# Holding back the last free buffer only when a transpose will soon need it

## The chip, the cores and the metric

The kernel runs on one core of a Trainium2 chip. The metric is the device time of one execution in microseconds; lower is better.

## What is computed

Four blocks follow one another on eight batch rows of one token each (448 features): attention A, mixer B, attention A, mixer B, with the same weights both times. Cut to what matters:

```python
q = (layernorm(x) @ wq)                       # 16 query heads of 256
scores = einsum("bhqd,bhkd->bhqk", q, k) * 256 ** -0.5   # 8 cached heads, 4096 keys, each for 2 query heads
o = einsum("bhqk,bhkd->bhqd", softmax(scores), v)
x = x + o @ wo                                # A
y = layernorm(x); x1 = y + mixed(gelu(layernorm(y) @ w1)) @ w2   # B; one token: the mixed part is zero
x = x + x1 + gelu(layernorm(x1) @ w3) @ w4
```

With one token a row, every shift in the mixing part shifts in zeros, so that term vanishes and `w1` and `w2` are not read. What is large is the cache: keys and values, 8 batch rows x 8 heads x 4096 x 256 in bf16 each.

## The kernel before

**Units, steps, parts.** A unit `t` is (pass, batch row, head): pass 1 is the first attention, pass 2 the second. `units` lists 144 of them in a hand-made order, gaps included: for each batch row the pass 1 heads, then a stretch with two gaps in which the dense layers between the attentions run (`mid_steps`, one piece a step), then at a unit called the fence the pass 2 heads. Each unit has four steps, `q` = 0 to 3, and the step number is `i = 4 * t + q`. A head's keys and values are cut in four parts of 512 KB each.

**Slots.** SBUF holds 31 slots of 512 KB (`slots`, parts of the tile `slab`). A part of K is loaded into a slot, transposed on VectorE from that slot into another one (`transposes`, two instructions at L562), and scored from there on TensorE (`k_part`, L653). A part of V is loaded and multiplied by the softmax weights (`v_part`, L630). The transposed keys of six heads a batch row stay in their slots from pass 1 to pass 2, except for two parts that are parked in PSUM (L567) and copied back by ScalarE (L520). So a K part takes one slot more for the time of its transpose, and gives back the slot it was loaded to.

**The list of loads.** `loads` is worked out beforehand: parts of K at the pace of `by`, parts of V at the step of their use in `plan` (some six steps after the unit's scores). `pump` takes loads from it while more than `RESERVE` = 1 slots are free, and issues them on SyncE's queue (L536). Two parts that follow each other go as one transfer of 1 MB, where the list and `take_two` allow it; where the pair can't be had and enough is under way, `pump` returns and waits for a pair of free slots. `pump` runs whenever a slot comes free: after a transpose, after the scores of a part that isn't kept, after a part of V. All of this happens while the program is built: on the chip, only the engines' orders and their waits are left, and a load waits for the last reader of its slot.

**Transposes.** At step `i`, `transposes` works off `todo` up to the number `by[i]`. A part that is not scored yet at this step can be put off: where it isn't loaded or no slot is free, the function returns and tries again at the next step.

**The softmax of a unit.** VectorE's reduce at L668 after the last scores, a broadcast on TensorE (L676), VectorE's reduce of the maximum at L686, exponentials on ScalarE (L689), sums and a reordering on TensorE (L702, L712), ScalarE's copies to `pt` (L720), VectorE's sum at L727 and a power on GpSimd (L731). These stand in the engines' orders among transposes, scores and values, at fixed steps.

Of the kernel before, what the change touches and what calls it, by code (L numbers as in the profile page):

```python
# [15 lines left out]
UNIT = 2048  # L16
N_SLOTS = 31
RESERVE = 1
KEEP = 6
PARKED = 2  # L20
RUN = 2
# [10 lines left out]
def kernel(  # L32
# [164 lines left out]
    def flush():  # L197
        while between:
            between.pop(0)()
# [162 lines left out]

    heads = list(range(G))
    loose = heads[: G - KEEP]

# [30 lines left out]
    def fresh(u, s):  # L398

        return u is not GAP and (u[0] == 1 or u[2] in loose)  # L400
# [4 lines left out]
    t = 0  # L405
# [21 lines left out]
    parts = [(t, s) for t in range(n_units) for s in range(4) if fresh(units[t], s)]  # L427
# [16 lines left out]
    for t in order:  # L444
        for s in range(4):
            i = late_v.get((t, s), 4 * t + s + LAG)
            if t in ends or units[t + 1 : t + 2] == [GAP]:
                i = 4 * t + (6, 6, 7, 7)[s]
            elif t + 2 == n_units:
                i = 4 * t + (7, 8, 8, 8)[s]  # L450
            elif t + 1 == n_units:
                i = 4 * t + (5, 5, 6, 6)[s]
# [3 lines left out]
    loads = []  # L456
# [5 lines left out]
    for i in range(4 * n_units + 8):  # L462
# [9 lines left out]
        t, q = divmod(i + 2, 4)  # L472
# [3 lines left out]
    free = list(range(N_SLOTS))  # L476
# [3 lines left out]
    def take():  # L480

        lone = [x for x in free if x ^ 1 not in free]
        x = min(lone or free)
        free.remove(x)
        return x

    def take_two():

        both = [x for x in free if x % 2 == 0 and x + 1 in free]
        if both:  # L490
            free.remove(both[0])
            free.remove(both[0] + 1)
        return both[:1]
# [13 lines left out]
    extra.append((w4_sb[:], B_w4.rearrange("(c p) d -> p c d", p=128)))  # L507
    n_loads = [0]

    def pump():  # L510
        while loads and len(free) > RESERVE:
            kind, t, i = loads[-1]
            _, b, g = units[t]
            if kind == "p":
                loads.pop()
                x = take()
                dst = slots[x].rearrange("p (e q c x) -> p q c e x", e=4, q=2, c=4)
                for j in range(2):
                    src = park[parked[g, i]][j][:].bitcast(BF16)
                    nc.scalar.copy(dst[:, j], src.rearrange("p (c e x) -> p c e x", c=4, e=4))  # L520
                kt_of[(1, b, g), i] = x
                continue
            cache, of = (A_k_cache, raw_of) if kind == "k" else (A_v_cache, v_of)
            n, two = 1, (kind, t, i + 1)
            if i % 2 == 0 and two in wide and two in loads[-PAIR_VIEW:]:
                x = take_two() if len(free) > RESERVE + 1 else []
                if x:
                    n, x = 2, x[0]
                    loads.remove(two)
                elif under_way[0] >= ENOUGH and two in firm:  # L530
                    return
            loads.pop()
            if n == 1:
                x = take()
            src = cache[b, g].rearrange("(p s e) d -> p s (e d)", s=4, e=8)
            nc.sync.dma_start(  # L536
                slab[:, UNIT * x : UNIT * (x + n)].rearrange("p (s d) -> p s d", s=n),
                src[:, i : i + n],
            )
            for m in range(n):  # L540
                of[t, i + m] = x + m
            under_way[0] += n
            n_loads[0] += n
            if n_loads[0] >= 8 and extra:
                nc.sync.dma_start(*extra.pop(0))

    todo = list(reversed(parts))

    def transposes(i):


        while len(parts) - len(todo) < by[i]:
            t, s = todo[-1]
            if 4 * t + s > i and ((t, s) not in raw_of or not free):
                return
            todo.pop()
            raw = raw_of.pop((t, s))
            kt = kt_of[units[t], s] = take()
            src = slots[raw].bitcast(FP32).rearrange("p (q c e i) -> p q c e i", q=2, c=4, e=4)
            dst = slots[kt].bitcast(FP32).rearrange("p (e q c r) -> p q c e r", e=4, q=2, c=4)  # L560
            for q in range(2):
                nc.vector.transpose(dst[:, q], src[:, q])  # L562
            _, b, g = units[t]
            if (g, s) in parked:
                for q in range(2):
                    dst = park[parked[g, s]][q][:].rearrange("p (c e r) -> p c e r", c=4, e=4)
                    nc.vector.transpose(dst, src[:, q])  # L567
            free.append(raw)
            under_way[0] -= 1
            pump()  # L570
# [12 lines left out]
    def make_blocks(t):  # L583

        if t in runs and t not in ready:
            p, b, g = units[t]
            if p == 1 or (b, g % 4 // 2) in q_done:
                x, n = runs[t]
                qT = qT1[:, :, b] if p == 1 else qT2[:, :, b % 2]
                expand(Qblk[x], qT[:, 4 * g : 4 * (g + n)], n, scb[t % 2])  # L590
                ready.add(t)
# [50 lines left out]
    def k_part(t, s):  # L642
        u = units[t]
        p, b, g = u
        if s == 0:
            assert t not in runs or t in ready
            scs[t] = scb[t % 2][:, 0:64].rearrange("p (c b h) -> p c b h", b=4, h=2)
        key = (u if fresh(u, s) else (1, b, g)), s
        ktv = slots[kt_of[key]].rearrange("p (e c m x) -> p e c m x", e=4, c=2, x=2)
        for c in range(2):  # L650
            for db in range(4):
                for x in range(2):
                    nc.tensor.matmul(  # L653
                        scs[t][:, 2 * s + c, :, :],
                        ktv[:, db, c, :, x],
                        Qblk[run_of[t][0]][:, run_of[t][1], db, x, :, :],
                        start=(db == 0 and x == 0),
                        stop=(db == 3 and x == 1),
                    )
        if p == 2 or g in loose or (g, s) in parked:  # L660
            free.append(kt_of.pop(key))
            pump()
# [9 lines left out]
    def max_mms(t):  # L672

        mzs[t] = scb[t % 2][:, 64:384]
        for h in range(2):
            nc.tensor.matmul(  # L676
                mzs[t][:, 128 * h : 128 * h + 128],
                pm[:, h : h + 1].to_broadcast([128, 128]),
                ident,
                start=True,  # L680
                stop=True,
            )

    def exps(t):
        mx = mzs[t][:, 0:256].rearrange("p (h n) -> p h n", h=2)
        nc.vector.tensor_reduce(nm, mx, AX.X, ALU.max, negate=True)  # L686
        pe = work.tile([128, 8, 4, 2], BF16, tag="pe", bufs=1)
        for h in range(2):
            nc.scalar.activation(  # L689
                pe[:].rearrange("p c b h -> p h (c b)")[:, h],  # L690
                scs[t].rearrange("p c b h -> p h (c b)")[:, h],
                ACT.Exp,
                bias=nm[:, h : h + 1],
            )
        pes[t] = pe
# [96 lines left out]
    for t in range(n_units + 1):  # L792
        cur = t < n_units
        for q in range(4):
            i = 4 * t + q
            if cur:
                if t in fence and q == 0:
                    flush()
                    while (fence[t], 1) not in q_done:
                        next(dense[0])  # L800
                        flush()
                    flush()
                    make_blocks(t)
                late = q == 0 and t and not beside[t]
                if beside[t]:
                    transposes(i)
                flush()
                if not late and not beside[t]:
                    transposes(i)
                if units[t]:  # L810
                    k_part(t, q)
            back = t and units[t - 1]
            if q == 0 and back:
                max_mms(t - 1)
                exps(t - 1)
            if cur and late:
                transposes(i)
            if back and q == 1:
                to_rows(t - 1)
                sums(t - 1)  # L820
            if q == 1 and not cur:
                mark(t - 2)
            for u, s in plan.get(i, []):
                v_part(u, s)
                if s == 3:
                    head_out(u)
            if q == 3 and cur and t > 1 and t - 2 not in ends:
                mark(t - 2)
            if q == 3 and t - 1 in ends:
                mark(t - 1)  # L830
            dense_next()
            if q > 1:
                make_blocks(t + 1)
            if cur and units[t] and q == 3:
                max_reduce(t)
# [112 lines left out]
```

## Time and profile before

| what | value |
|---|---|
| median of 3 runs | 1114.25 us (1113.67 to 1115.25) |
| the profiled execution, whole | 1115.99 us |
| its span, first to last instruction | 1114.2 us |
| granted TensorE clock | 1.00 |
| TensorE / VectorE / ScalarE / GpSimd busy | 687.9 / 550.7 / 306.0 / 104.1 us |
| read from HBM | 446.77 MB, 401 GB/s over the span |
| loads of V: 1 MB, 512 KB | 130 (13.1 us to landing), 252 (8.1 us) |
| loads of K: 1 MB, 512 KB | 97 (14.0 us), 126 (8.8 us) |
| one transpose instruction, L562 | 687 ns, two for each part |

The span is divided into 40 slices of 27.9 us; the profile gives the busy share of each engine and the GB/s of the load queue in each. The waits list says who waited, on what line, for whom, with the total, the number of times and the longest. In the timeline a row has the start, the duration, engine, line, operation, what is written and read, and in brackets the idle time ahead with what ended it. The chain lists, from the end backwards, the piece that held up the next one.

### The profile page before, as it was taken

Reading aid. Unit: us, or ns where it says so; the run is one execution under the profiler, and the core shown is the slowest. Engines: PE = TensorE matmul, PEld = TensorE weight load, DVE = VectorE, ACT = ScalarE, POOL = GpSimd, SP = SyncE. Lnnn points to the kernel's source line nnn. Section 1 sums busy time; section 2 is a strip of 40 time slices with the busy share of each in tenths; the row PEclk is TensorE's granted clock in tenths of the full one; section 3 lists DMA queues with packets and bytes.
Section 4 is the critical chain, followed back from the end, with each engine's and each line's share of the span. In section 5 each row is a group of like instructions: output and inputs, shape, how many; then the busy total and the mean of one; then the engine's idle time right before and its main releaser. Section 6 shows DMA issues by size and latency. Waiting matters only on the chain.

```text
span 1114.2 us, 46349 instructions
## 1 busy us (share of the span) xinstructions
PE 687.9 (62%) x20737; PEld 640.8 (58%) x20737; DVE 550.7 (49%) x1305; ACT 306.0 (27%) x1360; POOL 104.1 (9%) x156
## 2 busy tenths in 40 slices
PE   3345675666756576565756667565756667665766
PEld 2334565565646565565655556565656566555765
DVE  4347554654446445554455535563446535554322
ACT  1112124321233212422243212422143212422242
POOL 0001001110011100110011000110011000100011
DMA  9999999999999999999999999999999999999993
GB/s 367 394 418 425 408 417 422 424 417 395 417 423 424 400 403 419 423 424 391 414 420 424 402 410 404 420 424 415 383 421 424 409 412 404 422 423 400 371 405 128
DMA packets 94503, 449.77 MB, mean 404 GB/s; under 512 B 9936, under 2 KB 15968, under 8 KB 64864
## 3 DMA queue, kind: packets, MB, share of 16 engines
q1 hardware_dynamic: 94304, 446.81, 98.4%
q8 instruction: 162, 2.65, 0.9%
q14 instruction: 37, 0.30, 0.1%
HBM read 446.77 MB, written 0.01 MB: 401 GB/s over the span
## 4 chain that ended last, share of the span: by engine, by line
DMA 39%; PE 15%; issue 6%; ACT 6%; DVE 5%; POOL 0%; SPq 0%; DVEq 0%; ACTq 0%; POOLq 0%
DMA slab<-in_A_v_cache_dram 31%; DMA slab<-in_A_k_cache_dram 9%; PE bank L630 5%; PE bank L653 4%; DVE slab L562 3%; ACT pt L720 2%; PE bank L137 1%; ACT slab L520 1%; ACT pe L689 1%; DVE small L686 1%; PE bank L676 1%; PE bank L712 1%; ACT pt_far L720 1%; PE bank L702 1%; PE bank L313 1%
## 5 line engine op out<-in xcount | busy, mean ns | idle before, releaser
L562 DVE STREAM_TRANSPOSE slab<-slab 128x512 f32<-128x512 f32 x640 | 414.6, 687 | 214.7 <-DMA slab<-in_A_k_cache_dram 167.2
L630 PEld LDWEIGHTS <-slab 128*128 128x128 bf16 x8192 | 273.1, 106 | 286.5 <-DMA slab<-in_A_v_cache_dram 223.0
L630 PE MATMUL bank<-pt,slab 128*128 128x2 bf16 x7168 | 260.5, 166 | 232.7 <-DMA slab<-in_A_v_cache_dram 161.5
L653 PE MATMUL bank<-Qblk,slab 128*128 128x8 bf16 x8192 | 297.2, 168 | 77.4 <-DVE slab L562 39.1
L653 PEld LDWEIGHTS <-slab 128*128 128x128 bf16 x8192 | 267.8, 105 | 88.2 <-DVE slab L562 46.6
L689 ACT ACTIVATE pe<-bank,small 128x32 bf16<-128x32 f32 x256 | 61.3, 295 | 406.7 <-DVE small L686 406.7
L731 POOL TENSOR_TENSOR small<-small 128x2 f32<-128x2 f32 x112 | 78.2, 698 | 773.2 <-DVE small L727 773.2
L720 ACT CAST pt<-bank 32x64 bf16<-32x64 f32 x448 | 90.8, 203 | 106.4 <-PE bank L712 102.5
L686 DVE TENSOR_REDUCE small<-bank 128x2 f32<-128x256 f32 x128 | 54.1, 423 | 103.2 <-PE bank L676 102.9
L727 DVE TENSOR_REDUCE small<-bank 128x2 f32<-128x64 f32 x128 | 27.1, 212 | 118.5 <-ACT pt L720 102.9
L166 ACT CAST Qblk<-bank 32x32 bf16<-32x32 f32 (+1 forms) x272 | 48.2, 177 | 110.7 <-PE bank L160 108.2
L676 PE MATMUL bank<-rows,small 128*128 128x128 bf16 x256 | 48.5, 293 | 11.5 <-DVE small L668 11.5
L668 DVE TENSOR_REDUCE small<-bank 128x2 bf16<-128x64 f32 x128 | 26.4, 206 | 58.5 <-PE bank L653 58.3
L630 PE MATMUL bank<-pt_far,slab 128*128 128x2 bf16 x1024 | 37.0, 166 | 26.1 <-DMA slab<-in_A_v_cache_dram 24.4
L712 PE MATMUL bank<-pe,rows 128*128 128x64 bf16 x512 | 51.3, 241 | 1.9 <-issue 1.9
L712 PEld LDWEIGHTS <-rows 128*128 128x128 bf16 x512 | 33.8, 124 | 28.4 <-issue 28.1
L702 PE MATMUL bank<-pe,small 128*128 128x64 bf16 x128 | 27.3, 213 | 30.7 <-ACT pe L689 29.4
L182 PEld LDWEIGHTS <-wo_sb 128*128 128x128 bf16 x1152 | 35.5, 104 | 8.8 <-issue 7.7
L182 PE MATMUL bank<-OT,wo_sb 128*128 128x1 bf16 x1024 | 33.2, 165 | 5.6 <-ACT OT L599 4.5
L137 PEld LDWEIGHTS <-wq_sb 128*128 128x128 bf16 x864 | 30.6, 106 | 10.3 <-issue 5.9
L520 ACT COPY slab<-park 128x1024 bf16<-128x1024 bf16 x32 | 30.1, 1029 | 9.4 <-DVE slab L562 9.3
L599 ACT ACTIVATE OT<-bank,small 128x2 bf16<-128x2 f32 x122 | 25.4, 261 | 24.1 <-PE bank L630 22.7
(113 smaller groups left out, 386.5 us busy)
## 6 DMA issues: line engine op xcount, KB each, us to landing
slab<-in_A_v_cache_dram SPq DMA_DIRECT2D x130, 1024.0 KB, 13.1
slab<-in_A_v_cache_dram SPq DMA_DIRECT2D x252, 512.0 KB, 8.1
slab<-in_A_k_cache_dram SPq DMA_DIRECT2D x97, 1024.0 KB, 14.0
slab<-in_A_k_cache_dram SPq DMA_DIRECT2D x126, 512.0 KB, 8.8
wo_sb<-in_A_wo_dram SPq DMA_DIRECT2D x4, 896.0 KB, 11.7
wq_sb<-in_A_wq_dram SPq DMA_DIRECT2D x3, 1024.0 KB, 6.8
w_sb<-in_B_w_dram SPq DMA_DIRECT2D x1, 1568.0 KB, 12.5
w_sb<-in_B_w_dram SPq DMA_DIRECT2D x3, 448.0 KB, 16.7
```

The source lines that it names most:

```text
L137: nc.tensor.matmul(pv[:, i, j, :], cols(big[:, c, :], m + i * half), rows[:, c, :], start=(i == 0 and j == 0 and c == 0), stop=True, skip_ ...
L166: nc.scalar.copy(dst, src)
L182: nc.tensor.matmul(y[:, c, :], chunk(wo_sb[:, k, :], c), o[:, k, :], start=False, stop=True, skip_group_check=True,)
L562: nc.vector.transpose(dst[:, q], src[:, q])
L630: nc.tensor.matmul(pos[t][:, k, :], vv[:, c, 128 * k : 128 * k + 128], pts[t][:, 8 * s + c, :], start=(t == 0 and s == 0 and c == 0 and k ...
L653: nc.tensor.matmul(scs[t][:, 2 * s + c, :, :], ktv[:, db, c, :, x], Qblk[run_of[t][0]][:, run_of[t][1], db, x, :, :], start=(db == 0 and x ...
L676: nc.tensor.matmul(mzs[t][:, 128 * h : 128 * h + 128], pm[:, h : h + 1].to_broadcast([128, 128]), ident, start=True, stop=True,)
L686: nc.vector.tensor_reduce(nm, mx, AX.X, ALU.max, negate=True)
L689: nc.scalar.activation(pe[:].rearrange("p c b h -> p h (c b)")[:, h], scs[t].rearrange("p c b h -> p h (c b)")[:, h], ACT.Exp, bias=nm[:, ...
L712: nc.tensor.matmul(pp[:, c], sel, pe[:], start=True, stop=True)
L720: nc.scalar.copy(pts[t][sl].rearrange("p (k c) h -> p k c h", c=4), pp[sl, :, :, pb, :].rearrange("p c k h -> p k c h"),)
L731: nc.gpsimd.tensor_tensor(out=rz_of[t], in0=zs, in1=mone, op=ALU.pow)
```

## The change

`pump` asks a function `spare()` how many slots to hold back, where it took the constant `RESERVE`. `spare()` gives `RESERVE` (1) where the next part of K in `todo` is scored at most `SOON` = 4 steps after the present step, and 0 otherwise, so that a load may then take the last free slot. The same holds for pairs. The present step is kept in `now`, set in the main loop, and `todo` is made earlier, as `pump` reads it now.

```diff
 RESERVE = 1
+SOON = 4
...
+    now = [0]
...
+    todo = list(reversed(parts))
+
+    def spare():
+
+        return RESERVE if todo and 4 * todo[-1][0] + todo[-1][1] <= now[0] + SOON else 0
+
     def pump():
-        while loads and len(free) > RESERVE:
+        while loads and len(free) > spare():
...
-                x = take_two() if len(free) > RESERVE + 1 else []
+                x = take_two() if len(free) > spare() + 1 else []
...
-    todo = list(reversed(parts))
-
     def transposes(i):
...
-            i = 4 * t + q
+            i = now[0] = 4 * t + q
```

## The prediction

> **What bounds the kernel now.** I read the page first: the engines' shares, the forty slices, the queues and the chain that ended last.
>
> ```profile
> PE 687.9 (62%) x20737; PEld 640.8 (58%) x20737; DVE 550.7 (49%) x1305; ACT 306.0 (27%) x1360; POOL 104.1 (9%) x156
> ...
> GB/s 367 394 418 425 408 417 422 424 417 395 417 423 424 400 403 419 423 424 391 414 420 424 402 410 404 420 424 415 383 421 424 409 412 404 422 423 400 371 405 128
> ...
> q1 hardware_dynamic: 94304, 446.81, 98.4%
> ...
> DMA 39%; PE 15%; issue 6%; ACT 6%; DVE 5%; POOL 0%; SPq 0%; DVEq 0%; ACTq 0%; POOLq 0%
> ```
>
> No engine is over 62%, the load queue is at 98.4%, and the chain is mostly loads. The best slices move 425 GB/s, and once per batch there is a dip to 371 to 403. 446.8 MB at 421 GB/s (a usual good slice) would be 1061 us of the 1114.2 us span; ramp, tail and the dips are the rest. So the change counts only through what the load queue does: deeper queue, gain; a queue that runs dry, loss.
>
> From the issue times of the queue's timeline and the bytes of the packets I worked out how many 512 KB slots were issued and not yet landed at each moment, and the rate by that number: below 2 outstanding about 350 to 376 GB/s, 2 to 3 about 382, 3 to 4 about 393, 4 to 5 about 405, 5 to 6 about 412, 6 to 8 about 415, above 8 about 420. A slot takes 1.25 us at 420 GB/s.
>
> Then the queue's own waits, and one stretch of VectorE (batch 2, the steps after its fence, unit 50):
>
> ```profile
> SPq L536 <- PE bank L630: 202.2, 174, 5.0
> SPq L536 <- DMA slab<-in_A_v_cache_dram: 138.1, 120, 5.2
> SPq L536 <- DVE slab L562: 97.6, 49, 6.0
> ...
> ```
>
> ```profile
> 430.05 0.42 DVE L686 TENSOR_REDUCE small<-bank 128x2 f32<-128x256 f32 x1 [0.88 <-PE bank L676]
> 430.39 1.29 DVE L562 STREAM_TRANSPOSE slab<-slab 128x512 f32<-128x512 f32 x2
> 432.93 0.23 DVE L727 TENSOR_REDUCE small<-bank 128x2 f32<-128x64 f32 x1 [1.25 <-ACT pt L720]
> 433.19 1.30 DVE L562 STREAM_TRANSPOSE slab<-slab 128x512 f32<-128x512 f32 x2
> 435.40 0.23 DVE L668 TENSOR_REDUCE small<-bank 128x2 bf16<-128x64 f32 x1 [0.90 <-PE bank L653]
> 436.87 0.43 DVE L686 TENSOR_REDUCE small<-bank 128x2 f32<-128x256 f32 x1 [1.24 <-PE bank L676]
> 437.21 1.29 DVE L562 STREAM_TRANSPOSE slab<-slab 128x512 f32<-128x512 f32 x2
> ```
>
> and the chain there, where the next load of K waits for that last transpose:
>
> ```profile
> 437.29 1.22 DVE slab L562 x2
> ...
> 438.58 11.03 DMA slab<-in_A_k_cache_dram
> ```
>
> The reader is to see three things. A load waits for the last reader of its slot (TensorE at L630, VectorE at L562), or for a load to land: the trace has eight semaphores for these loads, used in turn, so a ninth waits for the first. A part costs VectorE two transposes, 1.3 us, and stands between the softmax reduces. And a load behind a late transpose is on the chain already.
>
> **What the change moves.** Following the kernel's own bookkeeping step by step for both versions (it is fixed at build time): TensorE's and GpSimd's instructions keep their order; loads keep their bytes, 605 become 607 (two pairs split). Three things move.
>
> 1. *One more slot under load.* In each batch the next K part is far off from about six steps before the fence to eight after it, so loads run one slot ahead for some 14 steps. In batches 0 to 3 five or six slots are outstanding there, issued every 1.24 us as an earlier one lands: the eight semaphores, not the slots, hold them back, and I take 0.3 us in all. In batches 4 to 7 only 2 to 4 are outstanding (the dense layers hold TensorE, and SP waits for slots). Windows over this stage: 411, 392, 403 and 370 GB/s for 30, 25, 23 and 24 us. Against 421 that is 0.7, 1.7, 1.0 and 2.9 us lost, and one slot can give back at most its own 1.25 us: 4.2 us at most. By the rate table one more slot gives 0.5 us a batch, 2.0 us. Gain 2.3 us, at most 5.2 (0.25 a batch more for batches 0 to 3).
>
> 2. *Six transposes wait and come at once.* With no slot left, each try to transpose ahead returns. In each of batches 0 to 6 the six parts of the eight steps after the fence are done together at the ninth step, where a load that waits for a pair leaves one slot free (in batch 7 two parts; a further part per batch moves one step, at nothing, as its keys are scored four steps later). On VectorE these twelve instructions stand behind the reduce of L686 of one unit, and ahead of the reduces L727, of the next unit's L668, and of two more transposed parts. For batch 2: start at 431.2 (first target free after the value matmuls of L630), 6 x 1.31 = 7.9 us, L727 0.2, one part 1.3: L668 starts at 440.7 instead of 435.40, 5.3 us late. TensorE, in order, stands at the broadcast of that maximum (L676), and the value parts and key parts queued behind it free their slots late; ScalarE's exponentials and copies follow it. The part after L686 ends at 443.4 instead of 438.5.
>  Cover: the loads outstanding. After the pair issued at 435.62 comes the pair that waits for that transpose, so nothing is issued for 7.8 us, and 7.2 slots outstanding shrink to 1.1 at 0.79 a us (415 GB/s). Some 5 us at 393 instead of 412 (0.25 us) and 2 us of refill at about 360 instead of 412 (0.25 us): 0.5 us.
>  The others the same way, from their own L686, transposes and issues. Batch 0: the pair issued at 170.7 waits for a part that ends at 175.6; 5.1 outstanding shrink to 1.2. Batch 1: 302.3 becomes 307.6, 5.6 to 1.4. Batch 3: 569.2 becomes 575.8, 6.4 to 1.2. Batch 6: 940.2 becomes 944.5, 4.9 to 1.5. With batch 2, five times 0.5 = 2.5 us. Batch 4: the next pair waits for keys scored behind the stalled broadcast, 695.6 becomes 700.7, from fewer slots: empty for about 0.4 us and then two more late loads, 1.4 us. Batch 5: free slots do not pair up, so a load issued at 815.1 in the profile waits until the part that ends at 824.5; 4.8 outstanding last to 821.3: empty for 3.2 us, and 0.8 us of low rate, 4.0 us. Batch 7: 0.2 us. Sum 8.1 us; from 4 (the queue never empties, 0.5 each) to 12 (refill twice as slow).
>  What VectorE gains earlier, its reduces freed of a transpose in front, is at most 0.6 us a unit and where SP waits for landings: nothing.
>
> 3. *Pairs fall otherwise* in the rest of a batch: loads stand 2 to 6 slots behind or ahead for a few steps, mostly with 5 to 10 outstanding. Step by step with the table: +0.9 and -2.2 us, so 1.3 us lost; taken from 2 gained to 4 lost. ScalarE's copies of parked parts (L520, 1.03 us each) move a step: nothing, ScalarE is at 27%.
>
> Sum: 8.1 - 2.3 + 1.3 = 7.1 us. The profiled execution took 1115.99 us (span 1114.2 and 1.8 around it), which would become 1123; on the median of 1114.25 the same sum gives 1121.3.
>
> A rule that speaks against the change: the Trainium skill, "Perfetto Trace Analysis", Optimizing Scalar/DVE Operations, says that where VectorE isn't saturated but causes bubbles on other engines, breaking up instructions may complete work sooner; this change does the opposite with whole groups. It gives no figure; by it alone the sign is a loss, as in my second step, and the row with VectorE at 49% is its case.
>
> **Rivals.**
> - *The bunch is hidden and the slot pays* (faster). The queue's depth decides: it holds if eight or so slots are outstanding when the six transposes begin, as nothing then runs dry in 7 us. The trace has 4.8 to 6.4 there, which speaks against it; for it speaks that the extra slot may raise this by one in batches 4 to 6. It gives 5.2 us: 1109. Chance 0.12.
> - *Neither shows* (within 0.2%, 2.2 us, about what a measurement of this kernel tells from no change): refill costs nothing, bunch 4, gain 4: 1114. Chance 0.13.
> - *Empty queues cost more*: each late load delays the values that TensorE waits for (L630 waits 186.0 us for them), and the delay comes back as later releases. Twice the bunch's price: 1129. Chance 0.08.
> - *TensorE slows down after the stall.* It now idles some 4.5 us seven times. Idle stretches up to 4.3 us (longest wait of L630's weight load) stand in the trace with the granted clock at 1.00 in all windows, which speaks against it. At half speed for three steps of 1.1 us matmul each, 3.4 us times 7 on top, half of it hidden: 1133. Chance 0.03. The Trainium skill, "TensorE: Matmul & The Clock Gate", Why this matters for your kernels, asks for no gaps over about 3 us, as one idle window halves the rate; this trace does not agree.
> - That the change does not do what it says is ruled out by the order of the built program: the six transposes stand together on VectorE in seven places.
>
> **How the numbers follow.** My forecast, slower by some 2 to 14 us (1116.5 to 1128), has the chance 0.64. Range: from gain 5.2 against bunch 4, 1113, to bunch 12 and pairs 4 less gain 2, 1128. It leaves out most of the faster case and the two dearest, about 0.2. Slower 0.64 + 0.08 + 0.03 = 0.75, within 0.2% 0.13, faster 0.12.
>
> **What would show it.** In the profile after: twelve L562's counterparts in a row (7.9 us) after the fence of batches 0 to 6; the next maximum's reduce 5 us later after the reduce of L686 than now; a pause in load issues of 7 us and more there, longest in batch 5, with GB/s under 390; in batches 4 to 7 a little higher GB/s in the 20 us before. I am wrong if those pauses stand beside an unbroken 410 GB/s, if the six transposes begin before that L686, or if the dense stage of batches 4 to 7 gains over 1 us each.

## The result, and the profile after

The changed kernel takes 1120.54 us (median of 6 runs, 1119.53 to 1121.84); beside it the kernel before took 1114.20 us (6 runs). The ratio is 1.0053, with a 95% interval of 1.0041 to 1.0064: slower by 5.9 us, 4.6 to 7.1. The forecast was 7.1 us slower. The profiled execution took 1119.53 us, with a span of 1117.8 us; the one shown of before took 1115.99 us, which is above its own median, so the two profiles lie only 3.5 us apart. Below, a ratio from a set of runs decides what a change is worth, and a single trace only shows where.

The new lines push the kernel's line numbers up by 6: loads are L544 now, transposes L568, values L636, key scores L659, and the softmax's reduces L674, L692 and L733. The page, with the lines that answer to those of before:

```profile
PE 690.3 (62%) x20737; PEld 641.9 (57%) x20737; DVE 551.2 (49%) x1305; ACT 306.8 (27%) x1360; POOL 104.4 (9%) x156
...
GB/s 366 395 418 425 411 414 407 424 420 399 416 418 423 415 399 412 425 423 399 416 406 425 422 412 410 388 424 419 416 332 424 421 411 407 400 424 413 386 409 121
...
q1 hardware_dynamic: 94592, 446.81, 98.0%
...
DMA 61%; PE 15%; DVE 9%; issue 7%; ACT 6%; SPq 2%; POOL 1%; DVEq 0%; ACTq 0%; POOLq 0%
```

No engine has more work. The load queue's share falls from 98.4% to 98.0%, VectorE's share of the chain rises to 9%, and one slice, the thirtieth (about 810 to 838 us, batch 5), moves 332 GB/s. The worst slice of before, ramp and tail aside, was 371. The queue's waits (who waited for whom: total, times, longest):

```profile
SPq L544 <- PE bank L636: 158.6, 149, 4.1
SPq L544 <- DVE slab L568: 150.4, 63, 8.4
```

Loads waited 97.6 us for transposes before, at most 6.0 us at a time; now 150.4 us, at most 8.4. VectorE in batch 2, the same stretch as was shown of before:

```profile
431.07 0.43 DVE L692 TENSOR_REDUCE small<-bank 128x2 f32<-128x256 f32 x1 [1.49 <-PE bank L682]
431.42 8.00 DVE L568 STREAM_TRANSPOSE slab<-slab 128x512 f32<-128x512 f32 x12
439.35 0.19 DVE L733 TENSOR_REDUCE small<-bank 128x2 f32<-128x64 f32 x1
439.45 1.29 DVE L568 STREAM_TRANSPOSE slab<-slab 128x512 f32<-128x512 f32 x2
440.66 0.19 DVE L674 TENSOR_REDUCE small<-bank 128x2 bf16<-128x64 f32 x1
...
441.68 1.29 DVE L568 STREAM_TRANSPOSE slab<-slab 128x512 f32<-128x512 f32 x2
```

These are the twelve instructions in a row, 8.00 us (forecast 7.9), and the next unit's maximum at 440.66 (forecast 440.7; 435.40 before). Between one unit's L692 and the next unit's L674 now stand seven parts where there were two. The dearest place is batch 5. Here is SyncE's queue, which starts its last load at 812.12 within the first row and its next one at 823.03:

```profile
812.12 11.24 SPq L544 DMA_DIRECT2D slab<-in_A_v_cache_dram  x2
823.40 0.52 SPq L544 DMA_DIRECT2D slab<-in_A_k_cache_dram  x1
```

and windows over that pause (length, busy time of each engine, granted TensorE clock, DMA share, GB/s):

```profile
811.50:819.50 8.00, 3.25 (x100) 2.91 (x98) 7.83 (x15) 1.71 (x8) 0.00 (x0) 1.00 0.97 393
819.50:823.00 3.50, 2.38 (x68) 2.23 (x67) 3.01 (x7) 0.60 (x3) 0.70 (x1) 1.00 0.24 92
823.00:826.00 3.00, 2.45 (x91) 2.39 (x87) 2.19 (x5) 1.77 (x10) 0.70 (x1) 1.00 0.54 139
826.00:829.00 3.00, 2.05 (x49) 1.51 (x45) 0.97 (x3) 0.91 (x5) 0.00 (x0) 1.00 0.99 374
```

The loads in flight last for some 8 us of the bunch (393 GB/s), then run out (92), and when issues start again it takes another 3 us to come back (139). Against 414 GB/s, what the kernel before moved from 805 to 830 us, this is 0.4 + 2.7 + 2.0 + 0.3 = 5.4 us in one place.

### The profile page after: what moved, and what is told of

Its sections match the earlier page's. It is cut to its first block, busy times and chain, and to the rows that moved or that the text cites. A ratio compares the mean times of both kernels' runs of the same rounds, so it can differ in the third digit from the quotient of the medians.

```text
span 1117.8 us, 46366 instructions
## 1 busy us (share of the span) xinstructions
PE 690.3 (62%) x20737; PEld 641.9 (57%) x20737; DVE 551.2 (49%) x1305; ACT 306.8 (27%) x1360; POOL 104.4 (9%) x156
## 4 chain that ended last, share of the span: by engine, by line
DMA 61%; PE 15%; DVE 9%; issue 7%; ACT 6%; SPq 2%; POOL 1%; DVEq 0%; ACTq 0%; POOLq 0%
DMA slab<-in_A_v_cache_dram 41%; DMA slab<-in_A_k_cache_dram 19%; DVE slab L568 6%; PE bank L636 5%; PE bank L659 3%; ACT pt L726 2%; ACT pe L695 1%; PE bank L682 1%; DVE small L692 1%; PE bank L138 1%; SPq L544 1%; ACT slab L528 1%; PE bank L718 1%; DMA wq_tl<-in_A_wq_dram 1%; ACT pt_far L726 1%
## 5 line engine op out<-in xcount | busy, mean ns | idle before, releaser
L568 DVE STREAM_TRANSPOSE slab<-slab 128x512 f32<-128x512 f32 x640 | 413.8, 687 | 192.7 <-DMA slab<-in_A_k_cache_dram 156.0
L636 PEld LDWEIGHTS <-slab 128*128 128x128 bf16 x8192 | 273.1, 106 | 254.3 <-DMA slab<-in_A_v_cache_dram 202.8
L636 PE MATMUL bank<-pt,slab 128*128 128x2 bf16 x7168 | 259.8, 166 | 202.6 <-DMA slab<-in_A_v_cache_dram 149.7
L659 PE MATMUL bank<-Qblk,slab 128*128 128x8 bf16 x8192 | 296.9, 168 | 97.4 <-DVE slab L568 39.1
L659 PEld LDWEIGHTS <-slab 128*128 128x128 bf16 x8192 | 268.8, 105 | 108.0 <-issue 59.4
L737 POOL TENSOR_TENSOR small<-small 128x2 f32<-128x2 f32 x112 | 78.4, 700 | 772.7 <-DVE small L733 772.7
L692 DVE TENSOR_REDUCE small<-bank 128x2 f32<-128x256 f32 x128 | 54.4, 425 | 105.6 <-PE bank L682 105.3
L674 DVE TENSOR_REDUCE small<-bank 128x2 bf16<-128x64 f32 x128 | 26.4, 207 | 105.9 <-PE bank L659 105.8
L733 DVE TENSOR_REDUCE small<-bank 128x2 f32<-128x64 f32 x128 | 26.9, 210 | 95.5 <-ACT pt L726 87.4
L636 PE MATMUL bank<-pt_far,slab 128*128 128x2 bf16 x1024 | 37.0, 166 | 24.4 <-DMA slab<-in_A_v_cache_dram 22.8
L138 PE MATMUL bank<-small,wq_sb 128*128 128x1 bf16 x768 | 28.0, 165 | 6.9 <-issue 6.9
```

Source lines behind the costliest of these rows:

```text
L138: nc.tensor.matmul(pv[:, i, j, :], cols(big[:, c, :], m + i * half), rows[:, c, :], start=(i == 0 and j == 0 and c == 0), stop=True, skip_ ...
L636: nc.tensor.matmul(pos[t][:, k, :], vv[:, c, 128 * k : 128 * k + 128], pts[t][:, 8 * s + c, :], start=(t == 0 and s == 0 and c == 0 and k ...
L659: nc.tensor.matmul(scs[t][:, 2 * s + c, :, :], ktv[:, db, c, :, x], Qblk[run_of[t][0]][:, run_of[t][1], db, x, :, :], start=(db == 0 and x ...
L737: nc.gpsimd.tensor_tensor(out=rz_of[t], in0=zs, in1=mone, op=ALU.pow)
```

## The experiments

Theory 1 is the prediction's: the bunch of transposes costs, and the slot gives little back. Theory 2 puts the loss on the slot or on how the pairs fall. Every kernel was timed in five rounds beside the kernel before; a time in us below is the ratio's excess times the median of before (1115.2 to 1115.6).

**e1: the bunch without the slot.** The kernel before, with the reserve as it was, and no transposes from the fence to the eighth step after it, so that the six come together at the ninth:

```diff
     def transposes(i):
+        if any(4 * f <= i <= 4 * f + 8 for f in list(fence)[:-1]):
+            return
```

> The kernel before with its one reserved slot, but the six transposes of the eight steps after the fence are put off to the ninth step in batches 0 to 6, as the change does; no load runs ahead. Theory 1 (the bunch is what costs): slower than before by more than the change is, about 8 to 13 us, as nothing is gained in return; issue pauses of 5 to 8 us after the fence. Theory 2 (the bunch is covered by outstanding loads, and the change loses by taking the last slot and by other pairs): within 2 us of before.

Measured 1121.84 us, ratio 1.0061 (1.0047 to 1.0076): 6.8 us slower. In its waits, loads behind transposes (here L563) rise from before's 97.6 us and 6.0 at most to

```profile
SPq L536 <- DVE slab L563: 123.7, 55, 7.8
```

The bunch alone, without any loan of the slot, makes the whole loss, though less than the 8 to 13 us of theory 1. Theory 2 falls as far as the slot goes; pairs fall otherwise here too.

**e2, e3, e8: the slot without the bunch.** The changed kernel with `SOON` = 12, 16 and 14: the reserve comes back before six parts have piled up.

```diff
-SOON = 4
+SOON = 12
```

> The changed kernel with SOON = 12 in place of 4: the slot is held back again from the fourth step after the fence, so loads still run one slot ahead from six steps before the fence, but at most two parts are transposed in one step. Theory 1: the loss goes and the gain stays, faster than before by 3 to 9 us (the profile of the changed kernel has its load queue catching up by 0.5 to 2.5 us ahead of each fence, some 10 us in all over the batches). Theory 2: still slower than before by 3 to 6 us, since the slot is still taken.

> SOON = 16: the slot is held back again from the fence on, the lead is kept only for the six steps before it. Theory 1: faster than before by 2 to 7 us, a little less than with 12, as the lead is shorter. Theory 2: slower by 2 to 5 us.

> The changed kernel with SOON = 14: no bunch, and the lead of one slot kept up to the second step after the fence, between e3 (16, no loss) and e2 (12, 2.3 us lost). Theory A (what the two differ in is how pairs and single loads happen to fall afterwards): no order with SOON, anywhere from 1113 to 1118, most likely like e3 at 1114 to 1115.5. Theory B (each further step of lead costs): between the two, 1115.5 to 1117.

Measured: e2 1.0020 (1.0011 to 1.0029), 2.2 us slower; e8 1.0010 (1.0000 to 1.0019), 1.1 us slower; e3 0.9992 (0.9984 to 1.0001), no difference that can be told from none. The gain that theory 1 had for e2 (3 to 9 us) and for e3 (2 to 7 us) is not there; both are misses for both theories. The three stand in order of `SOON`, as theory B of e8 had it, but e4 below keeps the slot on loan longer than all of them and loses nothing. What one trace of e2 shows is a single place: in batch 2 no load starts between 443.09 and 451.06 us. The bookkeeping has five to nine slots free there, but a pair must be an even slot and the one after it, and no such pair is free, so the load waits; 1.2 slots are left outstanding and 1.6 us are lost. Whether such places explain all of e2's 2.2 us is open.

**e4: the slot, and the bunch broken up.** The changed kernel, with at most one part transposed a step from the ninth to the fifteenth step after the fence:

```diff
     def transposes(i):
+        had = len(todo)
         while len(parts) - len(todo) < by[i]:
             t, s = todo[-1]
+            if len(todo) < had and any(4 * f + 8 < i < 4 * f + 16 for f in list(fence)[:-1]):
+                return
```

> The changed kernel with SOON = 4, but from the ninth to the sixteenth step after the fence only one part is transposed in a step; loads run ahead as in the change. Theory 1: most of the loss goes: from 5 us faster to 2 us slower than before, with no issue pause over 5 us. Theory 2: slower by 4 to 8 us, as with the change.

Measured 1114.48 us, ratio 0.9991 (0.9982 to 0.9999). The whole loss is gone, with the slot on loan as long as in the changed kernel and the same transposes as late or later. VectorE in batch 4 of e4 (transposes are L570, the maximum's two reduces L676 and L694, the sums L735):

```profile
688.40 0.43 DVE L694 TENSOR_REDUCE small<-bank 128x2 f32<-128x256 f32 x1 [0.99 <-PE bank L684]
688.75 1.30 DVE L570 STREAM_TRANSPOSE slab<-slab 128x512 f32<-128x512 f32 x2
690.91 0.23 DVE L735 TENSOR_REDUCE small<-bank 128x2 f32<-128x64 f32 x1 [0.86 <-ACT pt L728]
691.05 2.48 DVE L570 STREAM_TRANSPOSE slab<-slab 128x512 f32<-128x512 f32 x4
693.45 0.19 DVE L676 TENSOR_REDUCE small<-bank 128x2 bf16<-128x64 f32 x1
```

Three parts stand ahead of the next unit's maximum here, and it comes 5.1 us after L694. The expected "no issue pause over 5 us" is a miss, though: in this very batch no load starts between 690.80 and 698.50 us, where the next one waits for a pair, and 0.8 slots are left outstanding. But then four pairs go out within 2.7 us, and the landings fall only 0.6 us further behind those of the kernel before.

**e5, e6, e11: the bunch in some batches.** As e1, with the list of fences cut to batch 5, to batches 0, 1, 2, 3 and 6, and to batch 4:

```diff
-        if any(4 * f <= i <= 4 * f + 8 for f in list(fence)[:-1]):
+        if any(4 * f <= i <= 4 * f + 8 for f in list(fence)[5:6]):
```

> The kernel before with the bunch in batch 5 alone (no transposes in the nine steps from its fence). Theory 1 (the prediction's prices by batch: batch 5, where the load after the bunch finds an empty queue, is half of the sum): 3 to 5 us slower than before. Theory 2 (the prices are wrong by batch, every bunch costs about a seventh of the 6.8 us that all seven cost together): 0.5 to 1.5 us slower.

> The kernel before with the bunch in batches 0, 1, 2, 3 and 6 alone, priced at 0.5 us each. Theory 1 (those prices): 2.0 to 3.0 us slower than before. Theory 2 (every bunch costs the same): 4.3 to 5.5 us slower.

> The kernel before with the bunch in batch 4 alone. If the seven bunches add up, this has what e1 (6.8) leaves over e5 (0.2) and e6 (1.4): 4 to 6 us slower than before. If each bunch's price hangs on which slots happen to be free there (theory 3), there is no such sum, and it lies within 2 us of before; by the prediction's own price for batch 4, 1.4 us.

Measured: batch 5 alone 1.0003 (0.9995 to 1.0011), 0.3 us; the five others 1.0014 (1.0005 to 1.0023), 1.6 us; batch 4 alone 1.0033 (1.0019 to 1.0047), 3.7 us. Together 5.6, against e1's 6.8: they add up within the intervals, but neither by theory 1's prices nor by theory 2's equal ones. Batch 4 costs most and batch 5, priced at 4.0, nearly nothing. The traces show what differs. In batch 4 of e11 the queue starts nothing from 688.75 to 696.87 us, with 6.5 slots outstanding at its start and 0.3 at its end:

```profile
688.75 8.45 SPq L536 DMA_DIRECT2D slab<-in_A_v_cache_dram  x2
698.42 0.33 SPq L536 DMA_DIRECT2D slab<-in_A_k_cache_dram  x1
701.93 0.33 SPq L536 DMA_DIRECT2D slab<-in_A_v_cache_dram  x1
```

In the 5 us from 696.87 only three slots go out, where e4 started eight in half the time after a pause almost as long; 0.7 are outstanding at 701.93, and the landings fall 3.5 us further behind.

In batch 5 of e5 the same bunch stands on VectorE, but two slots side by side come free of TensorE's scores just as it begins. So a pair of 1 MB goes out at 813.80 (the second load of this row), and the pause after it is 5.8 us:

```profile
812.52 1.61 SPq L536 DMA_DIRECT2D slab<-in_A_v_cache_dram  x2
819.60 0.33 SPq L536 DMA_DIRECT2D slab<-in_A_k_cache_dram  x1
```

The changed kernel found no such pair there, waited with up to eight single slots free in the bookkeeping, and ran dry. A bunch has no price of its own: the price hangs on what is outstanding when it begins, on which slots it leaves free, and on how fast loads can follow it.

**e7: two groups of three.** e4 with a limit of three parts a step instead of one:

```diff
-            if len(todo) < had and any(4 * f + 8 < i < 4 * f + 16 for f in list(fence)[:-1]):
+            if len(todo) < had - 2 and any(4 * f + 8 < i < 4 * f + 16 for f in list(fence)[:-1]):
```

> The changed kernel, but the six transposes in two groups of three, at the ninth and the tenth step after the fence. Theory 1 (what counts is whether the loads outstanding outlast the pause, 7.2 or less at 0.79 a us): a pause of some 4 us leaves three or more outstanding in most batches, and the time is within 1 us of the fully spread kernel: 1113.5 to 1116. Theory 2 (the cost goes with the number of transposes that stand together): half of the loss stays, 1117 to 1118.5.

Measured 1122.06 us, ratio 1.0065 (1.0052 to 1.0078): no better than one group of six, which neither theory had expected. Its VectorE in batch 4 gives the likely reason, which e12 tests (lines as in e4):

```profile
689.59 0.43 DVE L694 TENSOR_REDUCE small<-bank 128x2 f32<-128x256 f32 x1 [1.00 <-PE bank L684]
690.40 3.98 DVE L570 STREAM_TRANSPOSE slab<-slab 128x512 f32<-128x512 f32 x6 [0.38 <-PE bank L638]
694.30 0.18 DVE L735 TENSOR_REDUCE small<-bank 128x2 f32<-128x64 f32 x1
694.41 5.00 DVE L570 STREAM_TRANSPOSE slab<-slab 128x512 f32<-128x512 f32 x8
699.33 0.19 DVE L676 TENSOR_REDUCE small<-bank 128x2 bf16<-128x64 f32 x1
```

The second half follows in the next step, with one short reduce between, so seven parts still stand ahead of the next L676, which comes 9.7 us after L694. No load started from 690.37 to 701.67.

**e9, e10: the bunch with a shorter wait for pairs.** Since waits for a pair show in batch 5 and in e7, the changed kernel (e9) and the kernel before (e10) let a load go alone, shortly after the bunch, where four slots are free:

```diff
+    def hurry():
+        return any(4 * f + 9 < now[0] < 4 * f + 16 for f in list(fence)[:-1])
...
-                elif under_way[0] >= ENOUGH and two in firm:
+                elif under_way[0] >= ENOUGH and two in firm and (len(free) < 4 or not hurry()):
```

> The changed kernel with the bunch left as it is, but in the tenth to fifteenth step after the fence a load no longer waits for a pair of slots where four are free: it goes alone. Theory 3 (the loss is made where the bunch falls together with a wait for a pair: slots lie free, none beside another, and the queue runs empty, as for 10.9 us in batch 5): most of the loss goes, 1113 to 1117. Theory 1 (the stalled softmax and the slots that come free late cost by themselves, pairs or not): 1118 to 1122.

> The kernel before with the same loosened wait for pairs and no bunch. Control for e9: if the wait costs only where a bunch stands before it, 1113.5 to 1116; if it costs in the kernel before too (its own dips to 383 to 403 GB/s), 1109 to 1113, and then e9 must be compared with this and not with the kernel before.

Measured: e9 1121.32 us, ratio 1.0059 (1.0045 to 1.0074), no better than the changed kernel; e10 1.0006 (0.9993 to 1.0018). So the wait for pairs costs nothing by itself. Whether the loss needs it beside a bunch (theory 3) is not settled by e9, as batch 4 shows. The queue, VectorE and TensorE read there (transposes L572, the maximum's reduces L678 and L696, sums L737, key scores L663, values L640):

```profile
690.62 9.41 SPq L548 DMA_DIRECT2D slab<-in_A_v_cache_dram  x2
700.12 0.38 SPq L548 DMA_DIRECT2D slab<-in_A_k_cache_dram  x1
```

```profile
690.36 8.00 DVE L572 STREAM_TRANSPOSE slab<-slab 128x512 f32<-128x512 f32 x12
698.28 0.19 DVE L737 TENSOR_REDUCE small<-bank 128x2 f32<-128x64 f32 x1
698.39 1.28 DVE L572 STREAM_TRANSPOSE slab<-slab 128x512 f32<-128x512 f32 x2
```

```profile
690.70 0.57 PE L663 MATMUL bank<-Qblk,slab 128*128 128x8 bf16 x16
...
691.37 0.59 PE L640 MATMUL bank<-pt,slab 128*128 128x2 bf16 x16
```

The next load, a single one, takes the slot that the seventh part gives back. That part ends at 699.67 and the load starts at 699.70, with nothing outstanding. But it was not the first slot to come free. By the kernel's bookkeeping, the scores and the values of the two TensorE rows gave back a slot each in the ninth step, by 692. There the load still waited for a pair: the edit reaches from the tenth step only, and asks for four free slots. When it went alone, `take` gave it the lowest-numbered single slot, that of the seventh part, and the two loads behind it in the queue, whose slots TensorE had long given back, started after it. A bunch with no wait for pairs at all, or with slots given in the order in which they come free, was not run. So whether a bunch would cost as much without that wait stays open.

**e12: three parts for each unit.** As e9, with the parts in threes at the ninth, thirteenth and seventeenth step, so that one group stands ahead of each maximum:

```diff
+            d = min((i - 4 * f for f in list(fence)[:-1] if i > 4 * f + 8), default=99)
+            if d in (10, 11, 12, 14, 15, 16) or (d in (9, 13, 17) and len(todo) < had - 2):
+                return
```

> The changed kernel with the parts done in threes at the ninth, the thirteenth and the seventeenth step after the fence, one group for each unit, so that three parts and not seven stand ahead of the next unit's maximum; loads go alone where four slots are free, as in e9, so that no wait for a pair comes into it. Theory 1, made sharper after e7 (what costs is the time that the transposes take ahead of the next unit's maximum, and in e7 the two halves stood ahead of the same one): 1114 to 1117. Rival (a group of three is already too much, as e7 seemed to say, or transposes done late cost by themselves): 1119 to 1122.

Measured 1117.80 us, just above the range of theory 1, beside 1115.59 for the kernel before; ratio 1.0011 (0.9998 to 1.0025), 1.2 us. Against e9, which has the same rule for pairs, most of the loss is gone. The groups of three are as long as e7's (L575 here; L681 is the maximum's first reduce, L740 the sums):

```profile
689.44 3.98 DVE L575 STREAM_TRANSPOSE slab<-slab 128x512 f32<-128x512 f32 x6
693.34 0.18 DVE L740 TENSOR_REDUCE small<-bank 128x2 f32<-128x64 f32 x1
693.45 0.21 DVE L681 TENSOR_REDUCE small<-bank 128x2 bf16<-128x64 f32 x1
```

but after each, the next maximum has its turn, 4.4 us after its L699. So it is not a group of three, nor a late transpose, that costs. What e4 and e12 have in common, and e7 and e9 lack, is that VectorE comes to the next unit's maximum in time. In e12 a load then goes out about every 1.25 us through the whole stretch; e4 has a pause, but slots enough right after it.

**All kernels together.** From issue times and packets, as in the prediction, I worked out for each trace how long fewer than two slots, and fewer than one, were outstanding (from 35 us to the last load):

| kernel | slower by, us | under 2, us | under 1, us |
|---|---|---|---|
| before | 0 | 6.6 | 0.4 |
| e4 / e3 | -1.0 / -0.9 | 4.4 / 4.1 | 0.3 / 0.7 |
| e5 / e10 | 0.3 / 0.7 | 5.9 / 4.2 | 0.3 / 0.1 |
| e8 / e12 | 1.1 / 1.2 | 8.6 / 3.8 | 1.1 / 0.0 |
| e6 / e2 | 1.6 / 2.2 | 6.9 / 7.9 | 0.5 / 0.8 |
| e11 (batch 4) | 3.7 | 12.5 | 2.7 |
| after | 5.9 | 17.1 | 6.0 |
| e9 | 6.6 | 13.7 | 6.2 |
| e1 | 6.8 | 13.9 | 2.8 |
| e7 | 7.2 | 14.8 | 6.7 |

Each kernel that loses over 3 us has 12 us and more under two slots, and no other has over 9. The order within either group is not explained by it, and each row rests on one trace.

## Why the prediction was right, and where it was not

The sign and the sum were right, and so was the main mechanism. That the sum came so near is in part luck. By the landings in the one trace of each, the changed kernel falls behind the kernel before by about 1, 0.5, 0.5, 1, 2, 6 and 2 us across the bunches of batches 0 to 6, some 13 in all, and is 3.0 behind at the end: it makes up some 10 us in between. The forecast had 8.1 lost there and 1.0 given back by the slot and the pairs together. Term by term:

**The bunch, with the pairs: 8.1 + 1.3 forecast.** e1 makes the same bunch without the slot, pairs falling otherwise included, and loses 6.8 us (5.2 to 8.5), less than 9.4. The times of the step held in six of the seven batches: the pair behind the bunch was forecast for 175.6, 307.6, 443.4, 575.8, 700.7 and 824.5 us in batches 0 to 5; it (or the load in its place) started at 175.91, 308.00, 443.06, 575.26, 698.75 and 823.03. Batch 6 went otherwise: a pair still went out at 940.66, and the next, forecast for 944.5, at 948.18. The signs named for it were met in batches 4 to 6, with pauses of 7.5 us and more and 355, 278 and 378 GB/s over the 16 us from 690, 811 and 940 us. In batches 0 to 3 the pauses are 5.6 to 7.6 us and the queue still moves 393 to 411 GB/s over 16 us, so there the bunch is mostly covered.

The price of it per batch was mis-sized, in two ways. The five cheap batches, 0.5 each, were too dear on the whole: 1.6 us for the five in e6 instead of 2.5. They run down to one or two slots but not dry. In the changed kernel's batch 6 even that was dear: with 1.0 slot left at the lowest, the queue moves 296, 359 and 326 GB/s in the three stretches of 3 us from 948 us, about 2 us lost. And running dry was too cheap. Batch 5 was put at 4.0 us, of which 3.2 with nothing outstanding; the windows show 5.4, because the restart (139 GB/s over 3 us) alone costs 2.0 where 0.8 was allowed for all of the low rate. Batch 4 was put at 1.4: alone it cost 3.7 in e11. The step that failed there is the refill, taken as 0.25 us: after the pause of e11 the slots come free too slowly to fill the queue again, and it moves 174, 350 and 240 GB/s from 697 to 699, 702 and 705 us. What the prediction did not say is that these prices belong to one arrangement of the slots: the same bunch in batch 5 costs 5.4 us in the changed kernel and 0.3 in e5.

**One more slot: gain 2.3 forecast.** Too much. e4 and e3 have the slot without the bunch and come out 1.0 and 0.9 us faster, with intervals from 2.0 to 0; the changed kernel loses 0.9 us less than e1 (5.9 and 6.8), inside both intervals. So about 1 us, if anything. The prediction named as a sign that it was wrong that the dense stages of batches 4 to 7 gain over 1 us each. By the landings in the one trace after against the one before, they do: the same bytes land 1.9 us earlier in batch 4, 2.5 in batch 5, 1.6 and 2.2 in 6 and 7, relative to the start of each stage. But this cannot be put down to the slot: e1, which lends none, makes up 1.8 us in batch 4 and 2.5 in batch 7 by the same count, and e5, which lends none and is hardly late, 2.2 in batch 7. So whether the ceiling of 1.25 us a batch held is not shown. Nor is an earlier landing a gain of time. In e4, which has no bunch, the landings of batch 5 run 1.4 us ahead over this stage, and 1.2 of it is gone eight steps after; in the changed kernel part of it makes up a lag left by the bunch of the batch before. The runs show the sum and not how much of the lead is used up by what; that division stays open.

**Pairs: 1.3 forecast, -2 to 4.** No experiment has it alone. e2 and e8, where nothing but `SOON` differs from e3, lie 2 to 3 us above it, so effects of that size occur; that they are the pairs' alone is not shown, and the sign in the changed kernel isn't known.

**The rivals.** That the bunch is hidden needed eight slots outstanding; 5.9 to 7.5 were, when the pauses of the seven batches began. (The "4.8 to 6.4" of that passage leaves out its own 7.2 of batch 2.) That late loads cost twice, through values that TensorE waits for, was too dark: landings behind by 5.1 us in batch 6 were 3.1 behind at the end. TensorE's slowing after a stall is shown wrong by the windows above: the granted clock is 1.00 in each of them, across a wait of 3.31 us,

```profile
819.61 0.57 PE L659 MATMUL bank<-Qblk,slab 128*128 128x8 bf16 x16 [3.31 <-DVE small L733]
```

and the sixteen products after it take 0.57 us, as the sixteen at 815.31 did. The Trainium skill ("TensorE: Matmul & The Clock Gate", Why this matters for your kernels) asks for no gaps over about 3 us; here the products after such a gap were as fast as those ahead of it.

**The rule on breaking up.** VectorE was busy 49% before and is so after, and where the same transposes stand in its order is worth 6.9 us (after against e4: 1.0053 and 0.9991), pairs that fall otherwise included (607 loads and 599). The Trainium skill ("Perfetto Trace Analysis", Optimizing Scalar/DVE Operations) says that breaking up instructions may complete work sooner where VectorE is not saturated but makes other engines wait; e4 points the same way, though it spreads a block of instructions and cuts none of them. e7 adds a bound: two halves with only a short reduce between them, and the awaited maximum behind both, cost as much as one block (1.0065).

## What to carry to other kernels

When a buffer is lent out until it is needed, look at what then happens all at once when it comes back: here six deferred transposes became 8 us on an engine that is half idle, ahead of a reduce that the other engines wait for. Price such a block by what is in flight when it begins and by how fast loads can follow it: where the loads outstanding outlasted the pause it cost from 0.5 to 2 us of landings here, and where they ran out, in batch 5, the gap and the restart came on top, some 6 us. And to break a block up, put the instruction that others wait for between the pieces; two pieces ahead of the same reduce gained nothing (e7). Last, look at which slot the load at the head of the queue was given: in e9 one slot that came free late held up loads whose own slots were free.

## What the runs showed of the hardware

- A load queue that has run dry needs longer to come back than I had thought: 139 GB/s over the 3 us after the first new issue, 374 over the next three, 424 in the following slice of 27.9 us. The Trainium skill ("SBUF — State Buffer", The DMA setup-cost knee) puts the fixed cost of a transfer at about 2 us, most of it at the completion. The 2.0 us lost in the first of these windows are of that size, but they lie at the start, where next to nothing moves until 823.9 us and loads go out one by one; no run here shows that the two are the same cost.
- Letting loads go sooner and in smaller pieces bought nothing in the kernel before: e10 makes 637 loads instead of 605, at 822 us with four slots more issued than before, and its time is the same (1.0006).
